# Windowed attention and a gated MLP on one core: token-wise casts, scores of two head pairs per visit, partial first sums

## The chip, the cores and the metric

The kernel runs on one core of one Trainium2 chip. The metric is the device time of one execution in microseconds (us). A core has a matmul engine (PE, with its weight loads shown as PEld), a vector engine (DVE), a scalar engine (ACT), a general engine (POOL), a queue-only engine (SP), and 16 DMA engines that all queues share.

## The reference, cut to what matters

```python
# q, k, v: (8 batches, 8 heads, 576 tokens, 64), float32
scores = (1 / sqrt(64)) * q @ k.transpose(0, 1, 3, 2)
rel = pos[:, None] - pos[None, :]
mask_plain = (rel >= 0) & (rel < 32)                        # heads 0..3
mask_dil = (rel >= 0) & (rel < 128) & (rel % 4 == 0)        # heads 4..7
attn = softmax(where(mask, scores, -1e9))
x = (attn @ v).transpose(0, 2, 1, 3).reshape(4608, 512)     # token rows
h = x @ w_in                                                # 512 -> 2048
g = h * sigmoid(beta * h)
out = g @ w_out                                             # 2048 -> 512, (4608, 512) float32
```

## The kernel before

**The MLP.** The 4608 token rows are cut into nine tiles of 512. A tile has 16 sums "h" (one for each 128 columns of `w_in`, four matmuls of 128x512, L824), each followed by a tanh on ACT (L831) and a gate on DVE (L836) that write `g`; then four blocks "o" of 128 rows (16 matmuls of 128x512 each, L856), evacuated by ACT or DVE and stored by SP. In tile 0 the first four h sums are done in two column halves (288 and 224), since the second half of batch 0's tokens comes later.

**The attention.** It writes `xT`, the transposed token rows that the h sums read. Batch b+1 is worked on while tile b is. Heads come in pairs. Pairs x = 0, 1 are the plain window: queries in 6 strips of 96, each strip against 128 keys. Pairs x = 2, 3 are the dilated heads, held by residue of the token number modulo 4, 128 tokens of each residue; the last 64 tokens of a batch (16 of each residue) are a separate small piece, the tail. The steps have names: `S..` scores, with exp on ACT and a 0/1 mask on DVE or POOL; `V..` values, with a normalisation on DVE; `T` and `U` scores and values of the tail; `X..` the way back into `xT`.

- Batches 0 to 2 (`DIRECT`): POOL loads q and k into `st` with a cast to bf16, PE transposes them (`KD QD KP QP`), ACT and DVE copy them to `dk dq kT qT`. Scores of pairs 0 and 1 are matmuls over 64 rows, two at a time on the two halves of the array (L678).
- Batches 3 to 7: POOL casts q and k to a DRAM scratch (L368, `s`), and SP reads it back with transposing DMAs (L417) into `dk`, `dq` and, for the plain heads, into `raw`. From `raw`, two copies spread the keys into `kz` (64 of its 128 rows are zero) and four copies spread the queries into `qd`. Scores of pairs 0 and 1 are then matmuls over all 128 rows (L703), four to a visit.
- The way back: batches 0 and 1 by PE transposes and copies (`X`), later ones by SP, which stores `xsp`, `xdm` and `xdt` to a DRAM tile and reads that back with a transposing DMA (L490). From batch 3 on the two halves of `xsp` are stored apart, and `xdt` in four pieces.

**The order.** All work is entered into a planner (`Plan.run`) with due times, costs of each engine and a number of PSUM banks by kind (`CAPS`). It writes out one fixed order for each engine, so each queue runs strictly in that order and waits where an operand is late. Where it believes PE idle early on it puts in filler matmuls on zeros (L968).

**Startup.** POOL issues the loads in one queue: q and k of batch 0, its v (`raw`, `vp`, `vt`), `w_in` in three pieces, batch 1's q and k, `w_out` in two pieces, batch 1's v. Masks are made on POOL in between.

Of the kernel before, what the change touches and what calls it, by code (L numbers as in the profile page):

```python
# [22 lines left out]
class Op:  # L23
    def __init__(self, engs, fn, deps, vt, acquire, group, dma, lat):
        self.engs, self.fn, self.vt, self.acquire = engs, fn, vt, acquire
        self.deps = [d for d in deps if d is not None]
        self.dma, self.lat, self.group = dma, lat, group
        self.end = self.ready = None
        self.waits = 0
        self.next = []  # L30
        for g in group if isinstance(group, list) else [] if group is None else [group]:
            g.users.append(self)


class Plan:
# [3 lines left out]
    CAPS = {"h": 3, "o": 2, "z": 4, "a": 8, "s": 5}  # L39
# [6 lines left out]
    def op(self, engs, fn, deps=(), vt=0.0, acquire=None, group=None, dma=0, lat=None):  # L46
        acquire = acquire if acquire is None or isinstance(acquire, list) else [acquire]
        o = Op(engs, fn, deps, vt, acquire, group or acquire, dma, lat)
        self.ops.append(o)
        return o  # L50

    def run(self, filler=None, filler_until=0.0):
# [13 lines left out]
        ends = []  # L66

# [19 lines left out]
        while n_left:  # L87
            best = None
            near = {}
            for o in avail:  # L90
                base = o.ready
                at = {e: max([free[e], base] + [t for x, t in o.group.read.items() if x != e]
                             if o.group is not None and e != "PE" else [free[e], base]) for e, d in o.engs}
                fin = min(at[e] + d for e, d in o.engs)
# [18 lines left out]
            if filler is not None and s <= filler_until and free["PE"] + 300 < s:  # L113
# [5 lines left out]
                free["PE"] = now + 225  # L119
                continue  # L120
# [6 lines left out]
            o.fn(e)  # L127
            free[e] = s + d
            o.start, o.end = s, s + d + self.LAT[e]
# [27 lines left out]
FIRST = "KD0 QD0 KD1 QD1 KP0 QP0 KP1 QP1 S2 S3 T S00 S10 V20 V21 V30 V31 U V00 V10 X2 X3 X00 X10 S01 S11 V01 V11 X01 X11"  # L157
LATER = "S2 S3 T V20 V21 V30 V31 U S00 S10 S01 S11 X2 X3 V00 V10 X00 X10 S02 S12 V01 V11 X01 X11"
# [3 lines left out]
def kernel(  # L162
# [35 lines left out]
    ADDED = 1  # L198
    BY_DMA = 2
    SPLIT = 4  # L200
# [16 lines left out]
    def copy(e, out, in_):  # L217
# [10 lines left out]
    mask_e = {n: const([P, 2, 2, 2, QT // 2], BF16, f"maske_{n}") for n in ("FP", "PP")}  # L228
# [14 lines left out]
    ptt = const([P, 2, 288], BF16, "ptt")  # L243
    ptt_own = ptt[0:2 * KTL][:, :, 0:256].rearrange(
        "p c (h s) -> p c h s", h=4)[:, :, :, 0:2 * UT]
# [9 lines left out]
    raw = const([P, 2, 4, S // 2], BF16, "raw")  # L255
    vd16 = raw[:].rearrange("p z h m -> p (z h m)")[:, 0:1024].rearrange("p (h T d) -> p h T d", h=4, T=C)
    vd16_of = [vd16] * DIRECT + [st[b % 2][:, 0:1024].rearrange(
        "p (h T d) -> p h T d", h=4, T=C) for b in range(DIRECT, B)]
    kT = [const([P, WIN + S], BF16, f"kT{x}") for x in range(2)]
    kz = const([P, 4, WIN + S], BF16, "kz")  # L260
    qd = const([P, 4, 2, S // 2], BF16, "qd")
    qT = qd[:].rearrange("p (x f) e m -> p x (f e m)", x=2)[:, :, 0:S]
# [27 lines left out]
    def t_fill1(e):  # L290
        for x in range(2):
            nc.vector.memset(kT[x][:, 0:WIN], 0.0)
            nc.vector.memset(qt[x][:], 0.0)
# [60 lines left out]
    def t_late(e):  # L354
        band(mask_d[:], [[0, 4]], [(1, P)], 0, WIN - 1, 1.0, 0.0)
        for n in ("PP", "FP"):
            band(mask_e[n][:].rearrange("p a b e m -> p (a b) e m"), [[0, 4]], [(1, 2), (2, QT // 2)],
                 WIN, -1, 1.0, 0.0)
            band(mask_n[n][:].rearrange("p a b n -> p (a b) n"), [[0, 4]], [(1, QT)], WIN, -1, 1.0, 0.0)
        nc.gpsimd.memset(mask_e["FP"][0:WIN, 0], 0.0)  # L360
        nc.gpsimd.memset(mask_n["FP"][0:WIN, 0], 0.0)
        nc.gpsimd.memset(kz[:], 0.0)  # L362
    late_fill = plan.op([("POOL", 11500)], t_late, vt=-.3)
# [17 lines left out]
    def plain_v(b, p0, c0):  # L381
        return bass.AP(tensor=v.tensor, offset=v[b, 0].offset + (p0 - WIN) * D + c0 * QT * D,
                       ap=[[D, (P if not p0 else P - WIN) if not c0 else WIN], [QT * D, 4 * NI - c0], [1, D]])

    def direct_vp(b, deps, vt):
        if b:
            return [load("POOL", (vp[b % 2][:, :, 0:D], plain_v(b, 0, 0)), deps, vt, 768, .27, 1450,
                         1100 if b < DIRECT else 4000)]
        return [load("POOL", (vp[0][WIN:P, :, 0:D], plain_v(0, WIN, 0)), deps, vt, 576, .25),
                load("POOL", (vp[0][0:WIN, 1:, 0:D], plain_v(0, 0, 1)), deps, vt, 184, .25)]  # L390

    def direct_vd(b, deps, vt, tdeps=()):
        src = v[b, 4:8].rearrange("h (t T) d -> t h (T d)", T=C)[0:P]
        out = [load("POOL", (vd16_of[b].rearrange("p h T d -> p h (T d)"), src), deps, vt, 512, .35)]
        for c in range(2):
            src = bass.AP(tensor=v.tensor, offset=v[b, 4].offset + ((P - WIN) * C + c) * D,
                          ap=[[2 * D, 2 * KTL], [S * D, 4], [1, D]])
            out.append(load("POOL", (vt_[b % 2][:, c, :, 0:D], src), list(tdeps), vt + (.15 if b == 0 else .02 if b < DIRECT else 0) + .001 + .001 * c, 96, .2))
# [4 lines left out]
    def cast(b, z, deps, vt):  # L403
        dst = scratch[b, z] = dram_pool.tile([2, S * 4 * D], BF16, name=f"s{b}_{z}")
        src = (k, q)[z][b].rearrange("(x h) s d -> x (h s d)", x=2)
        return load("POOL", (dst[:].rearrange("x (a e) -> (x a) e", e=1024),
                             src.rearrange("x (a e) -> (x a) e", e=1024)), deps, vt, 1152, .38)

    def crossbar(b, z, h0, deps, vt):
        flat = scratch[b, z][h0 // 4]  # L410
        if h0:
            dst = (dk, dq)[z][b % 2][:].rearrange("p r h t -> p r (h t)")
            src = flat.rearrange("(a e) -> a e", e=C * D)
        else:
            dst = raw[:, z].rearrange("p h m -> p (h m)").unsqueeze(1)
            src = flat.rearrange("(a e) -> a e", e=P)
# [31 lines left out]
    xcopy = {}  # L448

    def back_dma(b, j, vt_of, vdone):  # L450

        rows = dram_pool.tile([S // 2, HD], BF16, name=f"x{b}_{j}")
        plain = rows[:, 0:HD // 2].rearrange("(i m e) c -> e m i c", e=2, m=QT // 2)
        out = []
        if b < DIRECT:
            out.append(plan.op(
                [("SP", 500)], lambda e: nc.sync.dma_start(
                    out=rows[:, 0:HD // 2].rearrange("(i m) c -> m i c", m=QT),
                    in_=xsp[j][:].rearrange("p a x h d -> p a (x h d)")),
                [vdone[0, j], vdone[1, j]], vt_of[f"X1{j}"], dma=1200, lat=2000))  # L460
        for e_ in range(2 if b >= DIRECT else 0):
            out.append(plan.op(
                [("SP", 500)], lambda e, e_=e_: nc.sync.dma_start(
                    out=plain[e_], in_=xsp[j][e_ * QT // 2:(e_ + 1) * QT // 2].rearrange("p a x h d -> p a (x h d)")),
                [vdone[0, j], vdone[1, j]], vt_of[f"X1{j}"], dma=600, lat=2000))
# [7 lines left out]
        if j:  # L473
            for c in range(C):
                dil.append(plan.op(
                    [("SP", 500)], lambda e, c=c: nc.sync.dma_start(
                        out=right[t1 - t0:, c], in_=xdt[(c % 2 * 2 + c // 2) * UT:(c % 2 * 2 + c // 2 + 1) * UT].rearrange("p x h d -> p (x h d)")),
                    [vdone["U"]], vt_of["X11"], dma=150, lat=2000))
# [13 lines left out]
        for x in range(4):  # L492
            xcopy[b, x, j] = o

    def attention(b, ld, names, vts):
# [4 lines left out]
        if b < DIRECT:  # L500
            for n in [x for x in names if x[0] in "KQ"]:
# [8 lines left out]
                def evac(e, g=g, z=z, kind=kind, i=i):  # L510
                    tp = bank(g, BF16)[:, 0:S]
                    if kind == "P":
                        dst = qT[:, i] if z else kT[i][:, WIN:]
# [4 lines left out]
                key = (("kT", "qT")[z], i) if kind == "P" else (("dk", "dq")[z], kv, i)  # L518
                steps[n] = [plan.op([dve(S), act(S)], evac, [tr, fill1] + war(key), vt, group=g)]
                wrote(key)  # L520
        else:
            vt = vt_of["zPRE"]
            ready = {"D": [ld["x", 0, 4], ld["x", 1, 4]]}
            ops = []
            for e_ in range(2):
                def spread(e, e_=e_):
                    rows = slice(64 * e_, 64 * e_ + 64)
                    dst = kz[rows, :, WIN:].rearrange("p h (m e) -> p h m e", e=2)[:, :, :, e_]
                    copy(e, dst, raw[rows, 0])
                o = plan.op([("POOL", 1200), ("DVE", 1400)], spread, [ld["x", 0, 0], late_fill] + war("kz"), vt)  # L530
                used(("raw", 0), o)
                ops.append(o)
            wrote("kz")
            w = war("qd", ("qT", 0), ("qT", 1))
            for e_ in range(2):
                for half in range(2):
                    def spread(e, e_=e_, half=half):
                        copy(e, qd[64 * half:64 * half + 64, :, e_], raw[64 * e_:64 * e_ + 64, 1])
                    o = plan.op([("DVE", 900)] + ([("POOL", 1150)] if half == e_ else []), spread,
                                [ld["x", 1, 0]] + w, vt)  # L540
                    used(("raw", 1), o)
                    ops.append(o)
            wrote("qd", ("qT", 0), ("qT", 1))
            ready["P"] = ops


        def mixed(e):
            copy(e, dkt[kv][:], dk[kv][:, :, :, CT - KTL:].rearrange("p r h k -> p h k r"))
        o = plan.op([("DVE", 450), ("POOL", 500)], mixed,
                    (steps["KD0"] + steps["KD1"] if b < DIRECT else ready["D"][0:1]) + war(("dkt", kv)), vt_of["T"] - .01)  # L550
# [4 lines left out]
        for c in range(2):  # L555
            def padded(e, c=c):
# [3 lines left out]
            o = plan.op([("DVE", 250), ("POOL", 300)], padded,  # L560
                        (steps["QD0"] + steps["QD1"] if b < DIRECT else ready["D"][1:]) + [fill1] + war(("qt", kv)),
                        vt_of["T"] - .01)
# [8 lines left out]
        vdeps["P"] = ld["vp"] + [(fill3, fill4)[kv]]  # L571
        def spread(e):
            copy(e, vd[kv][:, :, :, 0:D], vd16_of[b])
        o = plan.op([("POOL", 1100), ("DVE", 620)], spread,
                    [ld["vd"][0], (fill3, fill4)[kv]] + war(("vd", kv)), vt)
# [7 lines left out]
        def exp_and_mask(key, sop, g, vt, n, sc, w, m, tiles):  # L583
# [4 lines left out]
            if b >= ADDED or key == ("T",):  # L588
                def mask(e):
                    E[e].tensor_tensor(out=w(), in0=w(), in1=m(), op=ALU.mult)  # L590
                ex = plan.op([("POOL", 120 + 2.2 * n), ("DVE", 160 + .65 * n)], mask,
# [410 lines left out]
```

The softmax here doesn't subtract the row's maximum and nothing guards it: scores larger than these inputs give would overflow.

## Time and profile before

| | |
|---|---|
| median of 13 runs | 311.62 us (310.5 to 312.5) |
| the profiled execution | 312.14 us |
| its span, first to last instruction | 310.4 us |
| granted PE clock, mean | 0.996 |
| busy PE / DVE / ACT / POOL | 96% / 64% / 55% / 35% of the span |
| HBM traffic | 39.32 MB read, 18.87 MB written |

The page is of the profiled execution. Sums in the prediction are made on its clock, in us from the start of its span. A PE row "x4" of the timeline is four matmuls that follow each other; the next row's start tells how long they took together, since the end of a matmul is modelled and overlaps the next. About one matmul record in fifty is missing from this trace, so a row "x3" of four equal matmuls is such a gap and no wait.

### The profile page before, as it was taken

Reading aid. Unit: us, or ns where it says so; the run is one execution under the profiler, and the core shown is the slowest. Engines: PE = TensorE matmul, PEld = TensorE weight load, DVE = VectorE, ACT = ScalarE, POOL = GpSimd, SP = SyncE. Lnnn points to the kernel's source line nnn. Section 1 sums busy time; section 2 is a strip of 40 time slices with the busy share of each in tenths; the row PEclk is TensorE's granted clock in tenths of the full one; section 3 lists DMA queues with packets and bytes.
Section 4 is the critical chain, followed back from the end, with each engine's and each line's share of the span. In section 5 each row is a group of like instructions: output and inputs, shape, how many; then the busy total and the mean of one; then the engine's idle time right before and its main releaser. Section 6 shows DMA issues by size and latency. Waiting matters only on the chain.

```text
span 310.4 us, 6029 instructions
## 1 busy us (share of the span) xinstructions
PE 296.7 (96%) x2270; PEld 153.3 (49%) x2307; DVE 198.8 (64%) x421; ACT 171.3 (55%) x302; POOL 108.4 (35%) x150
## 2 busy tenths in 40 slices
PE   6899999999999999999999999999999999999994
PEld 4565446554454445444454454445544444444453
DVE  4687968888958666875896868776863443333300
ACT  2667945866448555744674557455754544554311
POOL 8999654537170146315723751153000000000000
PEclk9999999999999999999999999999999999999998
DMA  6999999999779984999999859995024100001112
GB/s 96 172 209 207 206 187 204 235 154 171 156 165 173 190 166 108 164 149 192 203 185 172 207 116 167 129 247 126 22 61 112 47 34 34 36 34 56 45 70 70
DMA packets 93562, 42.49 MB, mean 137 GB/s; under 512 B 71052, under 2 KB 88220, under 8 KB 93212
## 3 DMA queue, kind: packets, MB, share of 16 engines
q0 software_dynamic: 42336, 19.66, 50.2%
q1 hardware_dynamic: 51052, 22.37, 35.5%
q8 instruction: 18, 0.29, 0.4%
q14 instruction: 12, 0.10, 0.1%
q10 hardware_dynamic: 144, 0.07, 0.1%
HBM read 39.32 MB, written 18.87 MB: 187 GB/s over the span
## 4 chain that ended last, share of the span: by engine, by line
PE 83%; POOL 7%; DMA 3%; DVE 3%; issue 2%; ACT 1%; POOLq 0%; ACTq 0%; DVEq 0%
PE bank L856 37%; PE bank L824 35%; DMA raw<-in_v_dram 3%; PE bank L703 2%; PE bank L755 2%; POOL st L368 2%; PE bank L740 1%; PE bank L644 1%; DVE g L836 1%; PE bank L434 1%; PE bank L725 1%; POOL kz L362 1%; DVE qt L218 1%; POOL vp L368 1%; PE bank L618 1%
## 5 line engine op out<-in xcount | busy, mean ns | idle before, releaser
L831 ACT ACTIVATE tnh<-bank,beta_half 128x512 bf16<-128x512 f32 (+2 forms) x148 | 100.1, 677 | 81.5 <-PE bank L824 72.9
L836 DVE SCALAR_TENSOR_TENSOR g<-tnh,bank 128x512 bf16<-128x512 bf16 (+2 forms) x148 | 98.8, 671 | 70.3 <-ACT tnh L831 69.1
L824 PE MATMUL bank<-xT,w_in_bf 128*128 128x512 bf16 (+2 forms) x576 | 139.8, 373 | 1.3 <-DVE xT L218 0.3
L856 PE MATMUL bank<-w_out_bf,g 128*128 128x512 bf16 (+1 forms) x571 | 137.7, 373 | 1.8 <-DVE g L836 0.5
L856 PEld LDWEIGHTS <-g 128*128 128x128 bf16 x592 | 55.4, 98 | 58.7 <-issue 0.8
L824 PEld LDWEIGHTS <-w_in_bf 128*128 128x128 bf16 x592 | 55.1, 98 | 58.3 <-issue 0.8
L873 ACT ACTIVATE osb<-bank 128x512 f32<-128x512 f32 (+2 forms) x36 | 21.0, 582 | 29.5 <-PE bank L856 24.5
L586 ACT ACTIVATE pt<-bank 128x384 bf16<-128x384 f32 (+1 forms) x54 | 22.1, 456 | 4.8 <-PE bank L703 3.5
L586 ACT ACTIVATE ptd<-bank 128x512 bf16<-128x512 f32 x32 | 17.0, 601 | 10.3 <-PE bank L644 10.3
L605 DVE TENSOR_TENSOR xsp<-bank,rcp 96x384 bf16<-96x384 f32 x32 | 17.7, 554 | 1.1
L604 DVE RECIPROCAL rcp<-bank 128x4 f32<-128x4 f32 (+2 forms) x72 | 12.8, 178 | 6.3 <-PE bank L740 3.7
L218 POOL COPY kz<-raw 64x1152 bf16<-64x1152 bf16 x6 | 9.4, 1570 | 19.7 <-DMA raw<-s 19.6
L590 DVE TENSOR_TENSOR ptd<-ptd,mask_d 128x512 bf16<-128x512 bf16 x24 | 13.1, 579 | 2.9 <-ACT ptd L586 2.6
L218 POOL COPY vd<-st 128x1024 bf16<-128x1024 bf16 x4 | 4.1, 1037 | 29.9 <-DMA st<-in_v_dram 29.9
L605 DVE TENSOR_TENSOR xdm<-bank,rcp 128x256 bf16<-128x256 f32 x32 | 13.6, 425 | 1.1
L590 POOL TENSOR_TENSOR pt<-pt,maske_FP 128x384 bf16<-128x384 bf16 x7 | 6.3, 912 | 21.1 <-ACT pt L586 13.1
L368 POOL DMA_DIRECT2D vp<-in_v_dram x9 | 11.9, 1327 | 2.6 <-DMA vp<-in_v_dram 2.6
L755 PEld LDWEIGHTS <-pt 128*128 128x128 bf16 x192 | 9.2, 97 | 6.5 <-issue 0.5
L755 PE MATMUL bank<-vp,pt 128*128 128x65 bf16 x192 | 10.6, 193 | 0.9 <-issue 0.4
L368 POOL DMA_DIRECT2D vt<-in_v_dram x16 | 10.9, 686 | 0.0
L875 DVE TENSOR_SCALAR osb<-bank 128x512 f32<-128x512 f32 (+1 forms) x2 | 1.0, 486 | 13.7 <-ACT osb L873 13.7
L218 DVE COPY qd<-raw 64x1152 bf16<-64x1152 bf16 x14 | 9.0, 642 | 0.2
(125 smaller groups left out, 221.9 us busy)
## 6 DMA issues: line engine op xcount, KB each, us to landing
out_dram<-osb SPq DMA_DIRECT2D x35, 256.0 KB, 2.0
s<-in_k_dram POOLq DMA_DIRECT2D x5, 576.0 KB, 7.6
s<-in_q_dram POOLq DMA_DIRECT2D x5, 576.0 KB, 10.2
vp<-in_v_dram POOLq DMA_DIRECT2D x7, 384.0 KB, 15.0
w_out_bf<-in_moe_w_out_dram POOLq DMA_DIRECT2D x2, 1024.0 KB, 17.0
st<-in_k_dram POOLq DMA_DIRECT2D x6, 288.0 KB, 13.4
st<-in_q_dram POOLq DMA_DIRECT2D x6, 288.0 KB, 13.6
x<-xsp SPq DMA_DIRECT2D x20, 72.0 KB, 2.3
```

The source lines that it names most:

```text
L218: (nc.scalar.copy if e == "ACT" else E[e].tensor_copy)(out=out, in_=in_)
L368: {"POOL": nc.gpsimd, "SP": nc.sync}[queue].dma_start(out=out, in_=in_)
L586: nc.scalar.activation(out=w(), in_=sc(), func=ACT.Exp, scale=SCALE)
L590: E[e].tensor_tensor(out=w(), in0=w(), in1=m(), op=ALU.mult)
L604: nc.vector.reciprocal(out=r, in_=p[..., D])
L605: nc.vector.tensor_tensor(out=dst, in0=p[..., 0:D], in1=r.unsqueeze(len(p.shape) - 1).to_broadcast(list(p.shape[:-1]) + [D]), op=ALU.mult)
L755: nc.tensor.matmul(pv[:, a, h2, :], lhsT=pt[x][:, (3 * j + a) * 2 + h2], rhs=vp[kv][:, (2 * x + h2) * NI + 3 * j + a, 0:D + 1], start=True ...
L824: nc.tensor.matmul(bank(g)[:, 0:n], lhsT=w_in_bf[:, kt, fb * P:(fb + 1) * P], rhs=xT[:, kt, xo:xo + n], start=(kt == 0), stop=(kt == NKT - 1))
L831: nc.scalar.activation(out=th[:, 0:n], in_=bank(g)[:, 0:n], func=ACT.Tanh, scale=beta_half[:, fb:fb + 1])
L836: nc.vector.scalar_tensor_tensor(out=g_t[t % 2][:, fb, c0:c0 + n], in0=th[:, 0:n], scalar=1.0, in1=bank(g)[:, 0:n], op0=ALU.add, op1=ALU.mult)
L856: nc.tensor.matmul(bank(g)[:, lo:hi], lhsT=g_t[t % 2][:, fb, tb * P:(tb + 1) * P], rhs=w_out_bf[:, fb, lo:hi], start=(fb == 0), stop=(fb = ...
L873: nc.scalar.mul(out=ob[:, cols], in_=bank(g)[:, cols], mul=0.5)
```

## The change

- **Casts and transposing reads, batches 3 to 7.** q and k are cast in halves by head group. For the dilated heads the scratch keeps its order. For the plain heads the scratch is written token by token (`(s h d)`: 2304 pieces of 64 elements), so that the transposing read gives `kT` and `qT` as the direct batches have them. `raw`, `kz`, `qd` and the six spreading copies go, and `kT` and `qT` are doubled.
- **Scores.** All batches use the 64-row matmuls. From batch 2 on (`PAIRED`) a visit does both pairs: 16 matmuls for the dilated heads, 12 and 12 for the plain ones, with four banks taken at once.
- **First sums.** In tile 0 the first four h sums are cut by rows of `w_in`: head pairs 2 and 3 first over all 512 columns, then pairs 0 and 1 in columns 0:288 and 288:512. The tail of batch 0 (`U`, and its way back as steps `Y2 Y3` of their own) comes after them, since tile 0 does not hold the tail's tokens. The tail's v load goes behind `w_in`, and batch 0's `vp` load is cut in three.
- **Stores.** `xsp` in one store for each half batch, `xdt` in one. The last output block is cut 256 + 128 + 128 columns, all stored by SP.
- **Masks and planner.** `mask_e` goes, the other masks are made in three separate steps, earlier; the planner's costs gain a price for changing between 64-row and 128-row matmuls and for DVE and POOL sharing SBUF access, and more DVE and less POOL masking results.

```diff
-FIRST = "KD0 QD0 KD1 QD1 KP0 QP0 KP1 QP1 S2 S3 T S00 S10 V20 V21 V30 V31 U V00 V10 X2 X3 X00 X10 S01 S11 V01 V11 X01 X11"
-LATER = "S2 S3 T V20 V21 V30 V31 U S00 S10 S01 S11 X2 X3 V00 V10 X00 X10 S02 S12 V01 V11 X01 X11"
+FIRST = "KD0 QD0 KD1 QD1 KP0 QP0 KP1 QP1 S2 S3 S00 S10 V20 V21 V30 V31 V00 V10 X2 X3 X00 X10 S01 S11 V01 V11 X01 X11 T U Y2 Y3"
+NEXT = "KD0 QD0 KD1 QD1 KP0 QP0 KP1 QP1 S2 S3 T S00 S10 V20 V21 V30 V31 U V00 V10 X2 X3 X00 X10 S01 S11 V01 V11 X01 X11 Y2 Y3"
+LATER = "S2 S3 T V20 V21 V30 V31 U S00 S10 X2 X3 V00 V10 X00 X10 S01 S11 V01 V11 X01 X11"
...
+    PAIRED = 2
     BY_DMA = 2
-    SPLIT = 4
+    APART = 4
...
-            out.append(load("POOL", (vt_[b % 2][:, c, :, 0:D], src), list(tdeps), vt + (.15 if b == 0 else .02 if b < DIRECT else 0) + .001 + .001 * c, 96, .2))
+            out.append(load("POOL", (vt_[b % 2][:, c, :, 0:D], src), list(tdeps), vt + (1.245 if b == 0 else .02 if b < DIRECT else 0) + .001 + .001 * c, 96, .2))
...
-    def cast(b, z, deps, vt):
-        dst = scratch[b, z] = dram_pool.tile([2, S * 4 * D], BF16, name=f"s{b}_{z}")
-        src = (k, q)[z][b].rearrange("(x h) s d -> x (h s d)", x=2)
-        return load("POOL", (dst[:].rearrange("x (a e) -> (x a) e", e=1024),
-                             src.rearrange("x (a e) -> (x a) e", e=1024)), deps, vt, 1152, .38)
+    def cast(b, z, h0, deps, vt):
+        dst = scratch[b, z, h0] = dram_pool.tile([S * 4 * D], BF16, name=f"s{b}_{z}_{h0}")
+        src = (k, q)[z][b, h0:h0 + 4]
+        if h0:
+            args = (dst[:].rearrange("(a e) -> a e", e=1024), src.rearrange("h s d -> (h s d)").rearrange("(a e) -> a e", e=1024))
+        else:
+            args = (dst[:].rearrange("(s h d) -> s h d", h=4, d=D), src.rearrange("h s d -> s h d"))
+        return load("POOL", args, deps, vt, 576, .38 if h0 else .25, 500 if h0 else 3000)
...
-            dst = raw[:, z].rearrange("p h m -> p (h m)").unsqueeze(1)
-            src = flat.rearrange("(a e) -> a e", e=P)
+            dst = qT[kv][:] if z else kT[kv][:, :, WIN:]
+        src = scratch[b, z, h0][:].rearrange("(a e) -> a e", e=C * D)
...
-        for e_ in range(2 if b >= DIRECT else 0):
-            out.append(plan.op(
-                [("SP", 500)], lambda e, e_=e_: nc.sync.dma_start(
-                    out=plain[e_], in_=xsp[j][e_ * QT // 2:(e_ + 1) * QT // 2].rearrange("p a x h d -> p a (x h d)")),
-                [vdone[0, j], vdone[1, j]], vt_of[f"X1{j}"], dma=600, lat=2000))
+        out = [plan.op(
+            [("SP", 500)], lambda e: nc.sync.dma_start(
+                out=rows[:, 0:HD // 2].rearrange("(i m) c -> m i c", m=QT),
+                in_=xsp[j][:].rearrange("p a x h d -> p a (x h d)")),
+            [vdone[0, j], vdone[1, j]], vt_of[f"X1{j}"], dma=1200, lat=2000)]
...
-            for c in range(C):
-                dil.append(plan.op(
-                    [("SP", 500)], lambda e, c=c: nc.sync.dma_start(
-                        out=right[t1 - t0:, c], in_=xdt[(c % 2 * 2 + c // 2) * UT:(c % 2 * 2 + c // 2 + 1) * UT].rearrange("p x h d -> p (x h d)")),
-                    [vdone["U"]], vt_of["X11"], dma=150, lat=2000))
+            dil.append(plan.op(
+                [("SP", 500)], lambda e: nc.sync.dma_start(
+                    out=right[t1 - t0:].rearrange("u c e -> c u e"), in_=xdt[:].rearrange("p x h d -> p (x h d)")),
+                [vdone["U"]], vt_of["X11"], dma=300, lat=2000))
...
-            for e_ in range(2):
-                def spread(e, e_=e_):
-                    rows = slice(64 * e_, 64 * e_ + 64)
-                    dst = kz[rows, :, WIN:].rearrange("p h (m e) -> p h m e", e=2)[:, :, :, e_]
-                    copy(e, dst, raw[rows, 0])
...
-            for e_ in range(2):
-                for half in range(2):
-                    def spread(e, e_=e_, half=half):
-                        copy(e, qd[64 * half:64 * half + 64, :, e_], raw[64 * e_:64 * e_ + 64, 1])
...
+            ready = {"D": [ld["x", 0, 4], ld["x", 1, 4]], "P": [ld["x", 0, 0], ld["x", 1, 0], fill1]}
...
+            if b >= PAIRED and x % 2:
+                continue
+            xs = (x, x + 1) if b >= PAIRED else (x,)
+            gs = [Group("s") for _ in range(2 * len(xs))]
...
+                for n, x in enumerate(xs):
                     for a in range(3):
                         i = 3 * j + a
                         for h in range(2):
                             rows = slice(64 * h, 64 * h + 64)
                             nc.tensor.matmul(
-                                bank(gs[h])[:, a * QT:(a + 1) * QT], lhsT=kT[x][rows, i * QT:i * QT + P],
-                                rhs=qT[rows, x, i * QT:(i + 1) * QT], start=b >= ADDED, stop=b >= ADDED or a == 2)
+                                bank(gs[2 * n + h])[:, a * QT:(a + 1) * QT], lhsT=kT[kv][rows, x, i * QT:i * QT + P],
+                                rhs=qT[kv][rows, x, i * QT:(i + 1) * QT], start=b >= ADDED, stop=b >= ADDED or a == 2)
...
-    def slot_h(t, fb, c0, n, vt, xdeps):
-        g = Group("h")
+    def slot_h(t, fb, c0, n, vt, apart):
+        g = Group("p" if apart else "h")
...
+        parts = [((2, 3), 0, n), ((0, 1), 0, S // 2), ((0, 1), S // 2, n)] if apart else [((0, 1, 2, 3), 0, n)]
```

## Prediction

> **What bounds the kernel now.** I read the page first: busy shares, slices, the chain that ended last.
>
> ```profile
> PE 296.7 (96%) x2270; PEld 153.3 (49%) x2307; DVE 198.8 (64%) x421; ACT 171.3 (55%) x302; POOL 108.4 (35%) x150
> PE   6899999999999999999999999999999999999994
> DMA  6999999999779984999999859995024100001112
> PE bank L856 37%; PE bank L824 35%; DMA raw<-in_v_dram 3%; PE bank L703 2%; PE bank L755 2%; POOL st L368 2%; PE bank L740 1%; PE bank L644 1%; DVE g L836 1%; PE bank L434 1%; PE bank L725 1%; POOL kz L362 1%; DVE qt L218 1%; POOL vp L368 1%; PE bank L618 1%
> ```
>
> PE is the bound: the MLP's 1152 matmuls of 128x512 start 216 ns apart, 248.8 us that the change does not touch. It can win only in the startup (first two digits, 6 and 8), in PE's attention work, in the few PE waits between, and behind the last matmul. The DMA row is 9 in most slices to about 210 us: a second resource with little room.
>
> Next the timeline around the first h sum.
>
> ```profile
> 19.61 0.10 PEld L824 LDWEIGHTS <-w_in_bf 128*128 128x128 bf16 x1
> 19.92 0.40 ACT L218 COPY xT<-bank 128x288 bf16<-128x288 bf16 x1 [0.33 <-DVE xT L218]
> 20.15 1.14 PE L824 MATMUL bank<-xT,w_in_bf 128*128 128x288 bf16 x8 [0.27 <-DVE xT L218]
> ```
>
> The weights are there at 19.61; the first sums wait for all four quarters of `xT`, until 20.15. The four early sums end at 24.67 (column half 224 from 23.91, eight more matmuls of 95 ns).
>
> PE's timeline around two score visits: a start less the one before is what a group took.
>
> ```profile
> 69.47 1.89 PE L824 MATMUL bank<-xT,w_in_bf 128*128 128x512 bf16 x8
> 71.29 0.43 PE L678 MATMUL bank<-qd,kT 64*128 64x96 bf16 x12
> 71.65 1.04 PE L824 MATMUL bank<-xT,w_in_bf 128*128 128x512 bf16 x4
> ...
> 99.67 0.33 PE L703 MATMUL bank<-qd,kz 128*128 128x96 bf16 x4
> 99.84 1.03 PE L824 MATMUL bank<-xT,w_in_bf 128*128 128x512 bf16 x4
> ```
>
> Eight h matmuls from 69.47 fill 8x216 ns, to 71.20; the next start at 71.65, so the 64-row visit of 12 costs 0.45. Visits of 6 (such as the one at 36.27) cost 0.33: about 0.20 for going over and back, and 21 ns a matmul. The four 128-row ones cost 0.17, 42.5 ns each, nothing fixed. So 64-row scores pay only in long visits.
>
> Then the rows around the longest late wait of PE.
>
> ```profile
> 172.51 1.65 DVE L218 COPY kz<-raw 64x1152 bf16<-64x1152 bf16 x1
> 174.79 2.24 DVE L218 COPY qd<-raw 64x1152 bf16<-64x1152 bf16 x3
> 174.93 0.40 PE L644 MATMUL bank<-dq,dk 64*128 64x128 bf16 x8 [0.46 <-DVE g L836]
> ```
>
> A gate stands in DVE's queue behind a 1.65 us spreading copy, and PE waits 0.46 for it. The like: 0.47 at 79.57 (gate), 0.41 at 197.60 (mask).
>
> Last, SP's queue and the DMA issues of batch 3.
>
> ```profile
> 62.03 2.02 SPq L417 DMA_TRANSPOSE dk<-s  x1
> 64.17 4.08 SPq L417 DMA_TRANSPOSE raw<-s  x1
> 68.30 2.58 SPq L417 DMA_TRANSPOSE dq<-s  x1
> 70.92 2.36 SPq L417 DMA_TRANSPOSE raw<-s  x1
> ...
> 80.46 3.04 SPq L490 DMA_TRANSPOSE xT<-x  x2
> ```
>
> SP runs in its order: what waits at a transposing read holds up stores and the `xT` reads behind it.
>
> **The change part by part.** Sums are in us against the profiled execution (312.14, span 310.4), which is 0.5 above the median; a difference is carried to the median unchanged.
>
> *Startup.* I replayed ACT in the new order from 10.98 with the old rows' durations (exps 0.52 from `ptd` to `ptd` and 0.33 from `pt` to `pt`, copies of 576 columns 0.63, of `xT` 0.35 to 0.40). Two `ptd` exps and three copies end at 13.93, two more `ptd` at 14.97, five `pt` at 16.62; X2's first copy then waits for its back transposes, whose bank comes free with a norm of DVE at 16.27, and ends at 17.05; with three more `pt` between, X3's copies end at 18.15 and 18.83. PE, with the last value matmuls of the first half at 19.3, starts the sums over pairs 2 and 3 there; pairs 0 and 1 then follow without a gap. Four sums are 16 matmuls of 512 columns, or 3.46 by 216 ns, plus 0.6 of transposes and values between them: they end at 23.4 against 24.67: 1.3 gained. A pessimistic replay (each hand-over between engines 0.2 later) starts at 20.15, ends at 24.2, and gains 0.5. The tail's U (0.40) and its way back (0.27) are not gone, only moved into dense PE time: −0.65. Waits of PE at 27.9, 32.9 and 40.36 (0.28, 0.33, 0.53; the last for POOL's `vd` copy after v lands at 39.22) shrink, since the loads keep their times while DVE takes the copy (0.47 against POOL's 1.04): +0.35. Net gain **1.0**, between 0.2 (pessimistic replay, and the w_out landing at 37.88 absorbs part) and 1.6. The two loads for the tail (0.52 in the queue) go behind `w_in`, whose first piece then lands near 18.9, still before 19.3.
>
> *Paired scores.* Both kernels' instruction orders give the visits. Batches 3 to 7: 24x42.5 ns = 1.02 becomes two visits of 12, 0.46 each, 0.92: 0.10 a batch, **0.5** in all (bounds 0.3 and 0.6); the dilated scores were already 16 in a row. Batch 2 had plain visits of 6, 6 and 12 (0.33+0.33+0.46) and dilated of 8 and 8 (0.42 each), and gets 12, 12 and 16 (0.46+0.46+0.65): 0.39 less. Batch 1 goes the other way, from 6, 6 and 12 to four of 6: 0.20 more. Net **0.2** (0 to 0.4). A paired visit needs four banks at once; banks for h wait if ACT is late. No row shows four taken together: between nothing and 0.3 a batch, and I take nothing, as ACT is 55% busy.
>
> *Spreading copies gone.* DVE loses 14 `qd` (0.642 mean, 9.0) and four `kz` (4.5), POOL about 16; DVE takes some 5.2 of masks from POOL and gives 1.2 back. DVE nets −9.5. Busy time off the bound costs nothing, but the gates behind these copies were late: the late waits (0.16, 0.16, 0.47, 0.46, 0.41 and small ones) come to 1.7. I take half, **0.8**, since a mask or norm before a gate can make the same wait; bounds: 1.6 gained, 1.5 lost to new ones (masks on DVE are 0.58 each).
>
> *Casts.* Page, DMA issues:
>
> ```profile
> s<-in_k_dram POOLq DMA_DIRECT2D x5, 576.0 KB, 7.6
> vp<-in_v_dram POOLq DMA_DIRECT2D x7, 384.0 KB, 15.0
> ```
>
> A linear half occupies the 16 engines for about 1.4 us. Token-wise it is 2304 packets of 128 bytes; the nearest row is `vp`, 3072 such packets, which pass at 1.2 to 2.84 ns each through the software queue: 2.8 to 6.5 us, about 2.9 more a half, 5.8 a batch. POOL's issue goes from 0.52 to about 1.2, on an engine that is idle. The queue is used for 18 us of a 31 us stage, and batches 4 to 7 are issued a stage ahead of need: cost nothing. Batch 3's alone has no lead: from the previous landing at 59.2, two linear halves 2.8, v 1.3, and 5376 packets (k 2304, v's tail 768, q 2304), so q lands at 63.3 + 5376p. SP then needs 2.4 for the read, 1.3 for stores, 1.75 to the second `xT` read and 4.5 for its landing, and tile 2's first h matmul (91.04 before, 89.5 in my sum) must not wait: q by 79.5, so p up to 3.0 ns. The rows give 70.0 to 78.6. Cost taken: **nothing**; bounds 0 and +5.
>
> These packets are written to DRAM, and no row shows 128-byte writes there; the 128-byte packets to SBUF took 32 ns, those of 512 bytes 59. [...]
>
> *Stores and the end.* Five SP issues fewer a batch (0.4 to 1.6 each), all in SP's slack. The last block's 256+128+128 columns by one queue: 0 to −0.2; taken as 0.
>
> Sum: −1.0 −0.2 −0.5 −0.8 = −2.5: 309.6 on the profile's clock, **309.1** for the median.
>
> **The rivals.** *No change, about 311.2.* The startup gain dies at the landing of `w_out` (37.88) and the stalls stay: −0.2 −0.5, and +0.3 for banks: 311.62−0.4. For it: the loads are back to back in one queue, so PE may only arrive earlier at the same wall. Against: 14 h sums fit before the first o, where 13 did.
>
> *Slower, about 313.3.* SP blocked at batch 3's `qT` read behind the token-wise cast, tile 2 late. It begins at 3.0 ns a packet, eats the whole gain at 3.5 (0.5x5.376 = 2.7), and gives +1.7 at 3.8 (4.2 late, less 2.5): 311.62+1.7 is 313.3. For it: 128-byte DRAM writes are unseen, and the queue's share rises while `xT` and stores share the 16 engines. Against: 2.84 is the worst row.
>
> **How the numbers follow.** Forecast case 0.66, no change 0.12, slower 0.22. The forecast case alone spans 307.2 (startup 1.6, stalls 1.6) to 310.9. The range goes to 312.8, into the slower case, to leave out no more than 2 in 10. 0.2% is 0.6 us, about what a measurement of this kernel can tell.
>
> **What would show it.** Right: first h matmul (now L808) near 19.3, four sums done near 23.4; plain score visits of 12 at about 0.46; no PE wait behind DVE near 80, 175, 198; q's cast landed before 79.5. Wrong: a PE wait of over 1 us near 90 ended by a DMA on `xT`; PE waiting on banks (ACT) around the paired visits; first sums at 20 or later.

## The result and the profile after

The changed kernel took 315.82 us (median of 11 runs, 313.59 to 318.2) against 311.78 before (48 runs): 1.0123 times as long, 95% interval 1.0101 to 1.0144. The forecast was 309.1, a gain; the kernel got slower. The ratios here leave disturbed executions out, so a ratio can differ from the quotient of the medians beside it. The profiled execution took 314.96, its span 313.2.

The page of the changed kernel (lines as those shown of before):

```profile
PE 296.3 (95%) x2275; PEld 150.3 (48%) x2312; DVE 182.5 (58%) x420; ACT 171.4 (55%) x315; POOL 89.1 (28%) x127
PE   7899999999966998999999999999999999999995
PEclk9999999999996999999999999999999999999999
DMA  6999999999999999699929999844034100000022
PE 77%; DMA 13%; DVE 4%; SPq 3%; issue 2%; ACT 1%; POOL 1%; POOLq 0%; DVEq 0%; ACTq 0%
```

DVE and POOL did get lighter, by 16 and 19 us, and the first digit of PE rose. But PE has a hole in slices 12 and 13, its clock a dip in slice 13, and DMA is 13% of the chain that ended last where it was 3%. Who was waited for, from the waits:

```profile
PE bank L808 <- DMA xT<-x: 5.7, 1, 5.7
PE bank L636 <- DMA dq<-s: 1.2, 1, 1.2
```

PE's timeline around the first of them:

```profile
90.28 0.81 PE L843 MATMUL bank<-w_out_bf,g 128*128 128x512 bf16 x3
96.81 3.46 PE L808 MATMUL bank<-xT,w_in_bf 128*128 128x512 bf16 x8 [5.71 <-DMA xT<-x]
```

PE is free for tile 2's first h sum at 91.1 and starts it at 96.8. The eight matmuls from there take 3.46 where eight such took 1.89 at 69.47 before. The granted clock explains it (one stretch; columns: length, busy time and count of PE, PEld, DVE, ACT, POOL; PE clock, DMA share, GB/s):

```profile
96.80:100.00 3.20, 3.19 (x8) 1.14 (x9) 0.51 (x1) 0.69 (x1) 0.80 (x1) 0.50 1.18 234
```

It is halved for some 3 us after the pause, which costs another 1.6. With the 1.2 before 118.94, PE loses 8.5 us.

Until there the changed kernel was ahead. Its startup:

```profile
18.70 1.03 PE L808 MATMUL bank<-xT,w_in_bf 128*128 128x512 bf16 x3
...
19.79 0.66 PE L808 MATMUL bank<-xT,w_in_bf 128*128 128x288 bf16 x4
```

First h matmul at 18.70 instead of 20.15; at the first o block (37.24 against 37.93) 14 h sums are done instead of 13, with the tail's U and its way back already behind. That is 0.69+0.86 = 1.55. But six fewer of batch 1's score matmuls are behind by then (42 against 48, a visit of 0.33), so the gain is about 1.2 net. The plain score visits:

```profile
67.92 0.81 PE L843 MATMUL bank<-w_out_bf,g 128*128 128x512 bf16 x3
68.66 0.43 PE L670 MATMUL bank<-qT,kT 64*128 64x96 bf16 x12
69.02 1.04 PE L843 MATMUL bank<-w_out_bf,g 128*128 128x512 bf16 x4
```

Three matmuls from 67.92 fill 3x216 ns, to 68.57; the next start at 69.02, so a visit of 12 costs 0.45, as priced. And no gate or mask of DVE makes PE wait near 80, 175 or 198.

Now POOL's queue, first in the changed kernel, where batch 4's loads begin at 75.41, then in the kernel of before, where they begin at 87.58:

```profile
74.83 0.63 POOL L232 COPY qt<-dq 64x128 bf16<-64x128 bf16 x2
75.41 0.57 POOL L381 DMA_DIRECT2D s<-in_k_dram  x1
...
80.79 2.52 POOL L381 DMA_DIRECT2D vp<-in_v_dram  x1
```

```profile
77.60 1.16 POOL L218 COPY qd<-raw 64x1152 bf16<-64x1152 bf16 x1
86.73 0.91 POOL L590 TENSOR_TENSOR pt<-pt,maske_FP 128x384 bf16<-128x384 bf16 x1 [7.97 <-issue]
87.58 0.57 POOL L368 DMA_DIRECT2D s<-in_k_dram  x1
```

Before, POOL sat 8 us in front of a mask of batch 3 that waited for its scores (their exp starts on ACT at 86.10), with batch 4's loads behind it. That mask and the spreading copies are off POOL's queue now, so the loads go 12 us earlier, into the time in which SP reads batch 2's `xT`. SP's queue of the changed kernel, columns start and duration:

```profile
76.88 0.54 SPq L472 DMA_DIRECT2D x<-xsp  x1
...
78.01 0.38 SPq L472 DMA_DIRECT2D x<-xsp  x1
83.95 5.77 SPq L499 DMA_TRANSPOSE xT<-x  x2
```

The stores are issued no later than before (76.88 and 78.01; before 78.06 and 79.50). But the reads wait until 83.95 for a store to land, and the last one, issued at 85.77, has landed only when PE starts at 96.8: 10.9 us, where the like read before took 3.9 (82.21 to 86.07). One stretch, 84 to 97, in the changed kernel and then before (columns as above):

```profile
84.00:97.00 13.00, 7.24 (x57) 3.34 (x58) 5.24 (x14) 3.56 (x10) 6.77 (x8) 0.85 1.87 160
```

```profile
84.00:97.00 13.00, 12.89 (x99) 6.84 (x100) 8.76 (x21) 6.96 (x12) 5.49 (x7) 1.00 0.85 155
```

Nearly the same bytes were moved. Batch 4's loads are in this stretch before as well, but they start at 87.58, when the reads of `xT` have landed. The share is the time that packets took, as a share of the 16 engines' time; it is no measure of the harm, since POOL's queue alone reached 2.17 with 128-byte packets (136.9 to 139.2 in the changed kernel). The packets of SP's reads show the harm: one of 256 bytes took 45 ns on average from 90 to 97, against 22.5 ns from 80 to 91 before. POOL's own 128-byte packets took 36 ns from 90 to 97, against 32 in that stretch of POOL's queue alone.

### The profile page after: what moved, and what is told of

The parts are those of the page before. It is cut to its first block, busy times and chain, and to the rows that moved or that the text cites. A ratio compares the mean times of both kernels' runs of the same rounds, so it can differ in the third digit from the quotient of the medians.

```text
span 313.2 us, 5987 instructions
## 1 busy us (share of the span) xinstructions
PE 296.3 (95%) x2275; PEld 150.3 (48%) x2312; DVE 182.5 (58%) x420; ACT 171.4 (55%) x315; POOL 89.1 (28%) x127
## 4 chain that ended last, share of the span: by engine, by line
PE 77%; DMA 13%; DVE 4%; SPq 3%; issue 2%; ACT 1%; POOL 1%; POOLq 0%; DVEq 0%; ACTq 0%
PE bank L843 37%; PE bank L808 32%; DMA vd<-in_v_dram 4%; DMA x<-xsp 4%; DMA dq<-s 3%; DMA st<-in_q_dram 2%; PE bank L726 2%; DVE g L822 1%; PE bank L670 1%; SPq L435 1%; PE bank L636 1%; PE bank L711 1%; PE bank L696 1%; PE bank L452 1%; POOL st L381 1%
## 5 line engine op out<-in xcount | busy, mean ns | idle before, releaser
L808 PE MATMUL bank<-xT,w_in_bf 128*128 128x512 bf16 (+1 forms) x565 | 140.3, 379 | 7.0 <-DMA xT<-x 5.7
L822 DVE SCALAR_TENSOR_TENSOR g<-tnh,bank 128x512 bf16<-128x512 bf16 x144 | 97.8, 685 | 78.4 <-ACT tnh L817 77.5
L817 ACT ACTIVATE tnh<-bank,beta_half 128x512 bf16<-128x512 f32 x144 | 98.5, 689 | 81.5 <-PE bank L808 76.6
L843 PE MATMUL bank<-w_out_bf,g 128*128 128x512 bf16 (+2 forms) x590 | 139.7, 368 | 1.4 <-issue 0.6
L858 ACT ACTIVATE osb<-bank 128x512 f32<-128x512 f32 (+1 forms) x36 | 21.2, 590 | 30.5 <-PE bank L843 29.7
L573 ACT ACTIVATE pt<-bank 128x288 bf16<-128x288 f32 x64 | 21.7, 417 | 7.7 <-PE bank L670 7.6
L381 POOL DMA_DIRECT2D s<-in_q_dram x10 | 13.1, 1307 | 1.8 <-DMA s<-in_q_dram 1.8
L381 POOL DMA_DIRECT2D s<-in_k_dram x10 | 11.1, 1106 | 0.0
L577 DVE TENSOR_TENSOR pt<-pt,maskn_FP 128x288 bf16<-128x288 bf16 x27 | 7.7, 316 | 5.3 <-ACT pt L573 5.3
L711 PEld LDWEIGHTS <-ptd 128*128 128x128 bf16 x128 | 6.8, 98 | 4.9 <-issue 0.2
## 6 DMA issues: line engine op xcount, KB each, us to landing
w_out_bf<-in_moe_w_out_dram POOLq DMA_DIRECT2D x2, 1024.0 KB, 16.3
```

Source lines behind the costliest of these rows:

```text
L381: {"POOL": nc.gpsimd, "SP": nc.sync}[queue].dma_start(out=out, in_=in_)
L573: nc.scalar.activation(out=w(), in_=sc(), func=ACT.Exp, scale=SCALE)
L711: nc.tensor.matmul(pv[:, r, a], lhsT=ptd[:, x - 2, j, 2 * r + a], rhs=vd[kv][:, 2 * (x - 2) + a, 2 * r + j, 0:D + 1], start=True, stop=True)
L808: nc.tensor.matmul(bank(g)[:, a:z], lhsT=w_in_bf[:, kt, fb * P:(fb + 1) * P], rhs=xT[:, kt, xo + a:xo + z], start=(i == 0 and kt == kts[0] ...
L817: nc.scalar.activation(out=th[:, 0:n], in_=bank(g)[:, 0:n], func=ACT.Tanh, scale=beta_half[:, fb:fb + 1])
L822: nc.vector.scalar_tensor_tensor(out=g_t[t % 2][:, fb, c0:c0 + n], in0=th[:, 0:n], scalar=1.0, in1=bank(g)[:, 0:n], op0=ALU.add, op1=ALU.mult)
```

## The experiments

Theory A: what hurts is that the loads of batches 4 and 5 are issued early. Rival B: the forecast's own slow case, SP's queue held up at batch 3's `qT` read. Within A, the shape of the packets may matter (A2) or not (A1).

**Loads held.** POOL's casts of batch b wait for `xT` of batch b−2:

```diff
+            if b > DIRECT:
+                c0 = (b - 2) * S
+                def seen(e):
+                    nc.gpsimd.tensor_copy(out=held[:, 0:2], in_=xT[:, 0, c0 + S // 2 - 1:c0 + S // 2 + 1])
+                behind = behind + [plan.op([("POOL", 120)], seen, xready(c0, c0 + S), b - 2 - .001)]
```

> Changed kernel, but POOL's loads of batch b (4 to 7) stand behind a two-column POOL copy that reads the xT of batch b-2, so that they are issued only when that xT has landed (before, they were issued at 87.6 for batch 4; in the changed kernel at 75.4). Theory A, early issue: the 5.7 us wait of PE for xT at 90.7, the slow matmuls behind it (1.6) and most of the wait at 117 (1.2) go, 306 to 308.5 us. Theory B, SP's queue: batch 3's four transposing reads stand ahead of the stores and of the xT reads whatever POOL does, the wait stays over 4 us, 314 to 316. Theory C, loads too late now: PE waits for dk or kT of batch 4 near 105, 310 to 314.

Measured: 307.71 against 311.18, ratio 0.9877 (0.9833 to 0.9921). From SP's and POOL's timelines:

```profile
77.95 0.33 SPq L473 DMA_DIRECT2D x<-xsp  x1
81.09 2.99 SPq L500 DMA_TRANSPOSE xT<-x  x2
```

```profile
86.35 0.19 POOL L918 COPY held<-xT 128x2 bf16<-128x2 bf16 x1 [10.53 <-DMA xT<-x]
```

SP's queue ahead of these reads is the same, yet they are issued 2.9 us sooner and have landed at 86.3, not 96.8. B falls, A holds; C (loads now too late) does not show. One wait of 1.5 for `xT` was left at 173.5, with batch 7's v loads issued at 164.4 ahead of the copy.

**Linear casts at the same early times.** `if h0:` in `cast` becomes `if True:`.

> Changed kernel in its own order and at its own issue times, but the casts of the plain heads are linear as those of the dilated heads (36 pieces of 18 KB instead of 2304 of 128 bytes), so the scratch of the plain heads of batches 3 to 7 has its numbers in another order and their scores are other numbers. Theory A1, what hurts is the early issue as such: the wait at tile 2 stays at 3 us or more, 313 to 316. Theory A2, what hurts is the early issue of many small packets: wait under 1.5, 307 to 310. Theory B, SP's queue: as A1, over 4 us.

The order of work stays; the trace has 16 pieces of 18 KB for a half, where 36 were expected. Measured: 329.07 (325.36 to 333.26), ratio 1.0524 (1.0449 to 1.06), above every range given. The profiled execution is the longest of the four (333.26, span 331.5), so its waits are too:

```profile
PE bank L808 <- DMA xT<-x: 23.9, 2, 20.2
```

So the small packets are not the culprit: with pieces of 18 KB, issued early, even the shortest execution (325.36) is longer than any of the changed kernel. A2 falls; A1 holds in that the wait is over 3 us, but with a price that I had not foreseen.

**Early casts put into the kernel of before.** Four casts into spare scratch behind batch 3's last copy on POOL:

```diff
+            for z in range(2 if b == DIRECT else 0):
+                for h0 in (4, 0):
...
+                    plan.op([("POOL", 400)], lambda e, args=args: dma("POOL", *args), ops, b - 1 + .01)
```

> Kernel of before with one addition: after batch 3's last copy on POOL (near 78.8) it issues four casts of batch 4's k and q into spare scratch that nobody reads, two linear halves and two token-wise halves, as the changed kernel does at 75.4 to 80.8 with those and v. Nothing else moves. Theory A, early issue: PE waits for xT at tile 2's first h sum (91.0) for 2 to 5 us, 313.5 to 317. Theory B, SP's queue: no such wait, 311 to 312.5.

Measured: 320.87 (316.29 to 325.11) against 311.18, ratio 1.0195 (1.0126 to 1.0264), the profiled execution 318.83 with a span of 317.1, and a wait at the same place, tile 2, now in the old kernel:

```profile
PE bank L831 <- DMA xT<-x: 3.9, 1, 3.9
```

The wait is in the 2 to 5 us expected, the time mostly above the 313.5 to 317. These casts come on top of batch 4's own loads, which the kernel issues again at 88.65, so the run shows that early casts make `xT` late and not what moving the loads costs.

**v's loads held too.** `behind[-1:]` is also added to what vd, vt and vp wait for.

> As the run with the held loads, but v's loads (vd, vt, vp) of batches 4 to 7 stand behind the same two-column copy too; there, batch 7's v loads had been issued at 164.4, ahead of the copy, and PE waited 1.5 us for xT at 173.1. Theory A, early issue: that wait goes, 305.5 to 307. Rival, v's loads are now late: PE waits for vd or vp of batches 4 to 7 by over 0.5 us in all, 307.5 or more.

Measured: 306.73 against 312.07, ratio 0.9844 (0.9804 to 0.9883), the fastest version; only the last run below is near it, and that one leaves out putting the plain heads' scratch in order. Its tile 2:

```profile
90.58 1.67 PE L809 MATMUL bank<-xT,w_in_bf 128*128 128x512 bf16 x7
```

No wait for a DMA at tile 2, and none over 0.5 later.

**First sums whole.** `APART = 0` in that version.

> As the run with all loads held, but tile 0's first four h sums are whole (no cut by rows of w_in); the order of the steps stays. If the first-sums part is worth what the prediction's startup term says (1.0 net), 0.5 to 1.6 us slower than the run with all loads held, and the first h matmul near 20.5 instead of 18.7. Rival, the walls at w_out and v's landing absorb it: within 0.3 us of that run.

Measured: 311.94 (ratio to before 0.9999, 0.9972 to 1.0026), 5.2 slower. The first h is at 20.61 instead of 18.06, so the wait for all of `xT` is back:

```profile
20.61 5.34 PE L809 MATMUL bank<-xT,w_in_bf 128*128 128x512 bf16 x24 [0.27 <-ACT xT L232]
```

By the first o block (37.57 against 37.05) that is 0.52 plus one sum (0.86) plus a visit of six score matmuls (36 of them done against 42, 0.33): 1.7, a little over the 0.5 to 1.6 expected. The planner also wrote another order, and four new waits of 0.8 to 1.1 (3.7 in all) stand at 58, 110, 144 and 175, two of them for `dq`. They come to about the rest of the 5.2, which is therefore not usable as a price of the first sums alone.

**One pair a visit.** `PAIRED = 9` in that version.

> As the run with all loads held, but each score visit does one pair: plain visits of 6 matmuls instead of 12, dilated ones of 8 instead of 16, two banks at once instead of four. By the visits' prices in the trace of before (0.33 for 6, 0.46 for 12, 0.42 for 8, 0.65 for 16): six batches times (4x0.33 - 2x0.46 + 2x0.42 - 0.65) = 3.5 us slower if all are kept apart, 1.5 to 3.5 where some stay next to each other. Rival, taking four banks at once holds up the h sums: under 0.5 us slower, or faster.

Measured: 309.32 (ratio to before 0.992), 2.6 slower. Some visits stayed next to each other; 20 more visits of 6 and four more of 8 replace ten of 12 and two of 16: 20x0.33−10x0.46+4x0.42−2x0.65 = 2.4. That is near the difference of the medians, but it isn't shown to be all of it: the planner wrote another order, a new wait of 1.1 for a load of q stands at 57.44, and the two profiled executions lie 4.3 apart (310.19 and 305.86). That four banks at once hold up the h sums does not show: in the version with all loads held PE has no wait over 0.3 from 25 us on.

**Only batch 4's loads held.** `if b > DIRECT` becomes `if b == DIRECT + 1`.

> As the first run with the held loads, but only batch 4's loads are held. Theory A, early issue, batch by batch: no wait at tile 2's first h sum (90.7); batch 5's loads (issued 89.4 in the changed kernel) now come right behind batch 4's and slow what SP reads near 105 to 120: a wait of 1 to 4 us there, 308 to 312. Rival, batch 4's loads alone do it: 306.5 to 308, as with all held.

Measured: 316.92, ratio 1.0164 (1.0121 to 1.0208). Tile 2 has no wait; batch 5's casts go at 101.42, and

```profile
115.91 1.04 PE L637 MATMUL bank<-dq,dk 64*128 64x128 bf16 x16 [5.97 <-DMA dq<-s]
```

Two more waits follow, 1.0 for `qT` at 125.6 and 1.9 for `xT` at 129.8. The wait moves to the reads of SP that are due next, as A says; it is longer than the 1 to 4 expected, and the time lies above the 308 to 312.

**The new last block alone, in the kernel of before.**

```diff
+        cuts = (0, HD // 2, 3 * HD // 4, HD) if last_one else (0, HD)
+        for i, (lo, hi) in enumerate(zip(cuts, cuts[1:])):
+            block_cols(t, tb, [x + i for x in vts], lo, hi)
```

> Kernel of before with only the changed kernel's last output block: cut 256 + 128 + 128 columns, each a PSUM group of its own, all stored by SP (before: 256 columns, then 256 in two halves, one stored by ACT's queue). From the start of the last matmul to the end of the span it took 4.7 us before and 3.5 in the changed kernel. If that is the cut and the queue, the span ends 1.0 to 1.3 us earlier, 310.4 to 311.0 against 311.6 to 312.1. Rival, the prediction's term: 0 to 0.2.

Measured: 311.38 against 311.64, ratio 0.9986 (0.9962 to 1.001), so no gain is clear of noise and the prediction's 0 to 0.2 fits. From the last matmul's start to the span's end it took 4.3, as in the old kernel with the extra casts (4.3; 4.7 in the profile before), and 3.5 in every version of the changed one. So the 0.7 to 1.2 that the changed kernel gains at its end is not the last block. It lies behind the last store's issue, which ends at 305.92 here (span 309.0) and at 310.90 in the changed kernel (span 313.2): 3.1 against 2.3. What makes that shorter stays open.

**Batch 3's masks back on POOL, nothing held.**

```diff
-                ex = plan.op([("POOL", 170 + 2.2 * n), ("DVE", 160 + .8 * n)], mask,
+                ex = plan.op([("POOL", 170 + 2.2 * n)] + ([] if b == DIRECT and key[0] in (0, 1) and not key[1] else [("DVE", 160 + .8 * n)]), mask,
```

> Changed kernel without held loads; only the four masks of batch 3's first half of plain scores are made on POOL instead of where the planner puts them, so that they stand in POOL's queue ahead of batch 4's loads, as a mask did in the kernel of before (86.7, loads from 87.6). If what lets the loads go early is only that nothing in POOL's queue waits any more: batch 4's loads are issued at 84 to 89, no wait over 0.5 us at tile 2's first h sum (90.7), and batch 5's then collide as in the run that holds only batch 4's: 314 to 317. Rival, some other change makes xT late: the wait at 90.7 stays over 2 us.

Measured: 320.47, ratio 1.0284 (1.0225 to 1.0343). POOL's and PE's timelines:

```profile
84.12 2.79 POOL L577 TENSOR_TENSOR pt<-pt,maskn_FP 128x288 bf16<-128x288 bf16 x4 [8.84 <-ACT pt L573]
88.16 0.73 POOL L577 TENSOR_TENSOR pt<-pt,maskn_PP 128x288 bf16<-128x288 bf16 x1 [1.25 <-ACT pt L573]
88.83 0.57 POOL L381 DMA_DIRECT2D s<-in_k_dram  x1
```

```profile
129.64 0.66 PE L670 MATMUL bank<-qT,kT 64*128 64x96 bf16 x12 [12.70 <-DMA qT<-s]
```

Five waiting masks (the four, and one at 88.16 that the planner added) are enough to move batch 4's loads to 88.83, and tile 2's wait is gone. Batch 5's go at 104.9, and PE waits 12.7 for batch 4's `qT`: the place was foreseen, the size not, and the time is above the 314 to 317.

**Linear casts, all loads held.** The edit of the second run in the held version.

> As the run with all loads of batches 4 to 7 held, but the plain heads' casts are linear (18 KB pieces), so their scratch of batches 3 to 7 has its numbers in another order and their scores are other numbers. It prices the token-wise cast by itself. If 128-byte pieces cost nothing that PE waits for once the loads are held: 306 to 307.5, as the run with all held (306.7). If they are what makes the loads long: 1 to 3 us faster. If 18 KB pieces are the worse neighbours of SP's reads even here: 1 us or more slower, with a PE wait ended by a DMA on dk, dq, kT, qT or xT.

Measured: 306.28, ratio 0.9829 (0.9779 to 0.9878), within 0.5 of the token-wise casts. Held, the shape of the casts costs nothing that PE waits for.

## Why the prediction was wrong, step by step

The step that failed is in the part *Casts*: "batches 4 to 7 are issued a stage ahead of need: cost nothing". Being early was taken for slack. It cost 8.5 us in the profiled execution (5.7+1.6+1.2), and 9.1 between the medians of the changed kernel and of the version with all loads held. One reading led there. POOL's masks and copies were counted as busy time that "costs nothing" when it goes, and "DVE takes some 5.2 of masks from POOL" stands in the sum, though the timeline of before showed what stood in front of the loads: 8 us of waiting at a mask. When the loads would go without it, and what early loads do to SP's reads, was not asked. The prediction's own sign of being wrong, a PE wait of over 1 us near 90 ended by a DMA on `xT`, came true.

The slow rival named the right victim, tile 2's `xT`, by the wrong agent. Batch 3's q cast landed at 72.03, inside the 70.0 to 78.6 worked out, which is 1.6 ns a packet and far from the deciding 3.0; SP issued its stores earlier than before. The rival did not reckon with the next batch's loads; that it has the right place and direction is luck.

The rest was right or too small. Startup: about 1.2 net against 1.0, inside its bounds. Paired scores: 0.45 a visit against 0.46. Copies off DVE: the three late waits (0.47, 0.46, 0.41) are gone; I took half of 1.7, and none of comparable size came in their place in the held version. DVE lost 16.3 us of busy time, not 9.5. The last block: nothing shown, as taken, but 0.7 to 1.2 was gained behind it that the sum does not have. POOL's issue of a token-wise half took 1.7 to 2.2 us (those issued at 76.47 and 79.69), not 1.2, and the wait put at 27.9 is at 28.6; neither changes the sum. With early issue out of the way the sum of −2.5 becomes −5.3 by the medians (306.73 against 312.07) and −4.9 by the ratio. That is at the forecast case's own lower end of 307.2, which the interval of the ratio takes in.

On the 128-byte packets into DRAM, which no row of before showed: in a stretch of the changed kernel with POOL's queue alone (136.9 to 139.2) 2294 of them started in 2.3 us, 1.0 ns each, and took 32 ns a packet, as into SBUF (32 in the trace of before). A half takes 2.3 us that way; of a linear half's 16 packets of 18 KB one took 1.38 us in the kernel of before (59 to 62). By the last run the shape is free in the held version (306.28 against 306.73).

## What to carry to other kernels

In a queue that runs in order, an instruction that waits is also a timer for the DMAs behind it (8 us of POOL at a mask, and batch 4's loads at 87.58; without it at 75.41); whoever moves it to another engine moves those DMAs, and must look for what is in flight at the new time. Slack on a prefetch does not make its issue time free: a load that nobody needs yet can still lengthen a transfer that PE needs now (the second read of `xT`: 10.9 us instead of 3.9). If the time of an issue matters, tie it to the data it should follow, and don't leave it to the masks that happen to precede it.

## What the runs showed of the hardware

- A second DMA queue at work slowed SP's reads without more being moved: with batch 4's loads beside SP's reads of `xT`, 84 to 97 moved 160 GB/s against 155 before, while a 256-byte packet of the reads took 45 ns instead of 22.5.
- Issued early, casts in 18 KB pieces held up SP's reads more than casts in 128-byte pieces (329.07 against 315.82 us; PE waits of 20.2 us, in the longest execution, against 5.7). Held, the two were equal (306.28 and 306.73).
- PE's pause of 5.7 us was paid for again by half the granted clock (eight matmuls in 3.46 instead of 1.89); the prediction's slow case left that out of its price. In the changed kernel the clock was 0.50 from 93.2, 2.1 us after the end of PE's last matmul (91.1), to 100.0, 3.2 us after PE's next start (96.8); the pause of 1.2 before 118.94 left it at 1.00. The mean of the profiled execution was 0.989, and 1.00 in the version with all loads held, where PE had no such pause.
